# One core, attention and a dense branch: an instruction order recorded by engine clocks, and single score blocks for VectorE

## The chip, the cores and the metric

The kernel runs on one core of one Trainium2 chip. Its time is the device time of one execution in microseconds (us), the median of several executions. Five engines work beside each other, each through its own list of instructions in order: TensorE (PE: matmuls; PEld: its weight loads), ScalarE (ACT), VectorE (DVE), GpSimd (POOL) and SyncE (SP, which here only issues transfers). They wait for each other through semaphores. Matmuls write to PSUM, which has eight banks of 128 partitions by 512 float32 values; everything else lies in SBUF.

## The reference

`x` is 2048 x 512. It is normalised row by row to `xn`. Two branches start from `xn` and meet at the end:

```python
q = (xn @ wq)            # 32 heads of 16 columns
k, v = xn @ wk, xn @ wv  # one k and one v of 16 columns, shared by all heads
p = softmax(q @ k.T / 4) # for each head: 2048 queries x 2048 keys
s = (p @ v for all heads) @ wo
g = silu(silu(xn @ w1) @ w2)   # w1 512 x 1792, w2 1792 x 512
out = x + s * g
```

There are 32 x 2048 x 2048 exponentials. They are most of the work, since each head has only 16 columns.

## The kernel before, in words

**Tiles.** The queries are cut into 4 chunks `c` of 512, the heads into 8 sets `g` of four, the keys into 16 tiles `kt` of 128. The 32 pairs (c, g) are called groups here. One score tile (c, g, kt) consists of four blocks, one for each head of the set. A block holds 128 keys on the partitions and 512 queries along the row, so it fills one PSUM bank. In all there are 32 x 16 = 512 tiles, or 2048 blocks. The four heads of a set use the four quarters of TensorE's rows (`burst`, L509), so that blocks of different heads run at the same time.

**Two ways to an exponential.** A tile of the A kind goes through `psA0` and `psA1`, two banks each: two blocks at a time are read by one ScalarE instruction (`emit_E`, L568) that writes 128 x 1024 values into one of 11 slots of `pa_sb`. A tile takes two such instructions. A tile of the D kind goes through `psD`, also two banks: VectorE adds a constant and converts to int16 (`emit_P1`, L581), which gives the bit pattern of a bfloat16 close to the exponential. It also takes two instructions a tile. GpSimd then makes two more patterns from the four blocks (`emit_shift`, two `int64_add` at L592), and the three patterns, weighted, give a better exponential. So a D tile has to be multiplied with the values three times, an A tile once.

**The value product.** `emit_PV` (L628) multiplies four blocks of four heads at a time with the values, on the four quarters of TensorE's columns, into bank `psO`. I call such a set of four matmuls a quad. An A tile costs one quad, a D tile three. When a group is complete, VectorE transposes the bank (`gn1`, L663) and normalises it in three or four further instructions (`gn2` to `gn4`).

**The dense work.** The query projections (`q`), first layer (`h`), second layer (`z`) and output projection (`w`, `wp`) are 104 jobs of 3 to 14 matmuls that all use the one bank `psF`. After an `h` or `z` job ScalarE takes a tanh of the bank (`emit_tanh`, L817) and VectorE multiplies tanh and bank (L858); after the others VectorE reads the bank once (L403, L866, L875). The bank is free for the next job only then.

**The order.** `Sched.op` records each instruction for its engine and works out the semaphore waits. The order on each engine is the order in which Python calls `op`. Before the change, this follows a fixed pattern. The 346 A tiles are the units of the loop `for u in range(NU)` (L887). A unit records two ScalarE exponentials (a tanh may come before either), VectorE's small tasks as far as a budget `room` of 0.85 or 1.3 us goes (L893), and one D instruction (L897); the two halves of a D tile fall to two units in turn. For each half unit TensorE gets the score blocks of the next unit (`emit_S`; the D blocks directly behind the second A pair of the unit) and then either a part of a dense job or up to `cap` quads (L913 to L928). Jobs have due units (`spread`, L695). The counts are fixed ahead (L490 to L497): from unit 12 (`NFRONT`) on, each unit carries half a D tile, which gives 166 D tiles. The first 12 units have none, since `psD` and VectorE still serve the layer norm, the keys and the values there. After the loop the last quads are recorded, then the last output projection, whose sums lie in `psA` (L939 to L970).

Of the kernel before, what the change touches and what calls it, by code (L numbers as in the profile page):

```python
# [6 lines left out]
ALU = mybir.AluOpType  # L7
# [28 lines left out]
class Sched:  # L36

    def __init__(self):
        self.queues = {}
        self.done = {}
        self.clock = {}
        self.snap = {}
        self.last_w = {}
        self.readers = {}
        self.flagged = {}
        self.lanes = {}

    def op(self, eng, fn, reads=(), writes=(), lane=None):
        who = lane or eng
        if lane:
            self.lanes[lane] = eng
        n = self.done.get(who, 0)
        self.done[who] = n + 1
# [15 lines left out]
        for w in writes:  # L72
            if w in self.last_w:
                dep(*self.last_w[w])
            for f, m in self.readers.get(w, {}).items():
                dep(f, m)
        clk = self.clock.setdefault(eng, {})
# [61 lines left out]
def bass_recurrent_scan__grouped_kv_mqa__dense_activation_silu__prompt_kernel(  # L139
# [32 lines left out]
    LEAD = 1  # L172
    NFRONT = 12

    with ExitStack() as es:
# [38 lines left out]
        scr_i = sb("scr_i", [P, 8], I16)  # L214
        psA = [es.enter_context(nc.psum_tensor("psA0", [P, 1024], FP32)),
# [16 lines left out]
        def load_x(a, b, queue="sp"):  # L232
            op(queue, lambda e: e.dma_start(x_sb[:, a:b, :], xv[:, a:b, :]), writes=[("x", t) for t in range(a, b)],  # L233
               lane=f"lx{a}")
# [7 lines left out]
        op("sp", lambda e: e.dma_start(wq_sb[:], A_wq.rearrange("(dc p) n -> p dc n", p=P)), writes=["wq"], lane="lwq")  # L242
# [22 lines left out]
        def warm(n, bank, key):  # L265
# [4 lines left out]
            op("pe", f, reads=["zero"], writes=[key])  # L270
# [119 lines left out]
        def mm_Q(c, t, dcs=range(NDC)):  # L390
# [5 lines left out]
            op("pe", f, reads=xnT_keys(c) + ["wq"], writes=["F"])  # L396

        def evac_Q(c, t, eng):
# [3 lines left out]
            else:  # L402
                op("v", lambda e: e.tensor_scalar(dst, psF[:, :], QSCALE, None, op0=ALU.mult), reads=["F"], writes=[("qT", c % 2, t)])  # L403
# [86 lines left out]
        units, dtiles = [], []  # L490
        for c in range(NC):
            for g in range(NG):
                n = 0
                while n < NKT and NFRONT + 2 * (len(dtiles) + n + 1) <= len(units) + (NKT - n - 1) - LEAD:
                    n += 1
                units += [(c, g, kt) for kt in range(NKT - n)]
                dtiles += [(c, g, kt) for kt in range(NKT - n, NKT)]  # L497
        NU = len(units)
        first_unit = [min(u for u, k in enumerate(units) if k[0] == c) for c in range(NC)]
        for u, k in enumerate(units):  # L500
            phase = (u - NFRONT) % 2
            m = (u - NFRONT) // 2
            d = dtiles[m] if u >= NFRONT and m < len(dtiles) else None
            units[u] = dict(phase=phase, pair=m, A=[[(k, 0), (k, 1)], [(k, 2), (k, 3)]][::1 if phase == 0 else -1],
                            D=[] if d is None else [(d, 0), (d, 1)] if phase == 0 else [(d, 2), (d, 3)])

        def score(e, blk, ap):
            (c, g, kt), i = blk
            return e.matmul(ap, lhsT=kT_sb[g % 2][32 * i:32 * i + 32, kt * P:(kt + 1) * P],  # L509
                            rhs=qT_sb[32 * i:32 * i + 32, c % 2, g // 2, :],  # L510
                            start=True, stop=True, tile_position=(32 * i, 0))

        def burst(items, writes):
            rd = set()
            for ((c, g, kt), i), _ in items:
                if ("q", c, g // 2) not in jst["q"]:
                    raise ValueError(f"no q for {c}, {g}")
                rd.add(("qT", c % 2, g // 2))
                rd.add(("kT", 1, kt // 2, i) if g % 2 else ("kT", 0, kt // 2 if kt else "first"))

            def f(e):
                for blk, ap in items:
                    r = score(e, blk, ap)
                return r
            op("pe", f, reads=sorted(rd, key=str), writes=writes)

        def emit_S(u, which):

            un = units[u]
            burst([(blk, psA[which][:, 512 * k:512 * k + 512]) for k, blk in enumerate(un["A"][which])], ["A%d" % which])  # L530
            if which == 1 and un["D"]:
                burst([(blk, psD[:, 512 * k:512 * k + 512]) for k, blk in enumerate(un["D"])], ["D", "D1"])

        NGRP = NC * NG
        pend = [[] for _ in range(NGRP)]
        left = [0] * NGRP
        for un in units:
            for blk in un["D"]:
                left[blk[0][0] * NG + blk[0][1]] += NPH
            for h in range(2):  # L540
                for blk in un["A"][h]:
                    left[blk[0][0] * NG + blk[0][1]] += 1
        npv = [[0] * 4 for _ in range(NGRP)]
        tot = [[0] * 4 for _ in range(NGRP)]
        for un in units:
            for blk in un["D"]:
                tot[blk[0][0] * NG + blk[0][1]][blk[1]] += NPH
            for h in range(2):
                for blk in un["A"][h]:
                    tot[blk[0][0] * NG + blk[0][1]][blk[1]] += 1  # L550

        step_now = [0]
        state = dict(g=0, o_step=-1, half=0)

        def fresh(key):
            for q in pend:
                for p in q:
                    if p["key"] == key:
                        raise ValueError(f"{key} is still to be read, step {step_now[0]}")

        def emit_E(u, h):
            un = units[u]
            if not un["A"][h]:
                return
            sl = (2 * u + h) % NPA
            step_now[0] = 2 * u
            fresh(("pa", sl))
            op("a", lambda e: e.activation(pa_sb[:, sl, :], psA[h][:, :], ACT.Exp, scale=ESCALE),  # L568
               reads=["A%d" % h], writes=[("pa", sl)])
            for k, (kk, i) in enumerate(un["A"][h]):  # L570
                gi = kk[0] * NG + kk[1]
                pend[gi].append(dict(i=i, kt=kk[2], v=0, ap=pa_sb[:, sl, 512 * k:512 * k + 512], key=("pa", sl),
                                     ready=2 * u + h))

        def emit_P1(u):
            un = units[u]
            if not un["D"]:
                return
            sl, h = un["pair"] % NPD, un["phase"]
            fresh(("ph", 0, sl, h))  # L580
            op("v", lambda e: e.tensor_scalar(ph_sb[0][:, sl, 1024 * h:1024 * h + 1024], psD[:, :],  # L581
                                              float(PH_ONE + PH_BIAS), 0.0, op0=ALU.add, op1=ALU.max),
               reads=["D", "D1"], writes=[("ph", 0, sl, h)])
            for k, (kk, i) in enumerate(un["D"]):
# [423 lines left out]
```

## Time and profile before

| | |
|---|---|
| median of three runs | 696.19 us (695.96 to 696.57) |
| span of the profiled execution, first to last instruction | 695.3 us |
| granted TensorE clock, mean | 1.000 |
| ScalarE, busy | 677.0 us (97%) |
| TensorE, busy by the records | 677.3 us (97%) |
| VectorE, busy | 552.4 us (79%) |
| GpSimd, busy | 352.3 us (51%) |
| ScalarE exponentials (L568) | 692, mean 1233 ns |
| VectorE pattern instructions (L581) | 332, mean 1221 ns |
| GpSimd shifts (L592) | 332, mean 1038 ns |
| tanh (L817) | 72, mean 824 ns |

The whole execution is a little longer than the span of its instructions. The busy time of an engine is the time covered by at least one of its records. Records overlap: on ScalarE and TensorE an instruction starts while the one before it is still in the pipeline, so the number of instructions times the mean duration is more than the busy time. What one more instruction costs is read from the distance between the ends, or the starts, of neighbours.

### The profile page before, as it was taken

What the parts mean: (1) busy time and instruction counts of PE and PEld (TensorE: products, weight loads), DVE (VectorE), ACT (ScalarE), POOL (GpSimd) and SP (SyncE); (2) the same over time, 40 slices, a digit from 0 to 9 for tenths busy, and PEclk for the clock granted to TensorE, in tenths of its full rate; (3) what the DMA queues carried; (4) which work ended last, traced back from release to release, by engine and by line L of the source; (5) the groups of instructions that cost most, each with busy time, mean ns of one, the idle gap of its engine ahead of it and who ended that gap; (6) DMA issues with size and microseconds to landing.
All of it is one profiled execution on the core that took longest, in us unless ns stands there. A gap on an engine that the chain in (4) does not pass through costs nothing.

```text
span 695.3 us, 14435 instructions
## 1 busy us (share of the span) xinstructions
PE 677.3 (97%) x6279; PEld 183.0 (26%) x6279; DVE 552.4 (79%) x639; ACT 677.0 (97%) x773; POOL 352.3 (51%) x361
## 2 busy tenths in 40 slices
PE   8999999999999999999999999999999999999996
PEld 3432222222222222222222222222222222222221
DVE  6778778887778877888778787887878888787884
ACT  5899999999999999999999999999999999999995
POOL 4134545545455555555555555455545555555452
PEclk9999999999999999999999999999999999999999
DMA  9300000000000000000000000000000000000000
GB/s 296 112 5 1 1 2 1 1 1 2 1 1 8 9 1 9 8 2 1 1 1 10 8 8 1 10 1 1 1 2 1 8 17 2 9 1 2 1 1 31
DMA packets 7887, 10.13 MB, mean 15 GB/s; under 512 B 1744, under 2 KB 7120, under 8 KB 7824
## 3 DMA queue, kind: packets, MB, share of 16 engines
q1 hardware_dynamic: 6656, 5.15, 2.4%
q0 software_dynamic: 736, 3.67, 1.5%
q8 instruction: 49, 0.80, 0.5%
q10 hardware_dynamic: 432, 0.39, 0.2%
q14 instruction: 14, 0.11, 0.1%
HBM read 6.85 MB, written 2.10 MB: 13 GB/s over the span
## 4 chain that ended last, share of the span: by engine, by line
ACT 93%; PE 4%; DVE 1%; DMA 1%; POOL 0%; SPq 0%; issue 0%; DVEq 0%
ACT pa_sb L568 87%; ACT t_sb L817 5%; DMA wq_sb<-in_A_wq_dram 1%; PE psA L509 1%; PE psF L268 1%; PE psD L316 1%; DVE stats_sb L277 0%; PE psO L628 0%; POOL rstd_sb L286 0%; PE psD L351 0%; PE psF L351 0%; PE psA L939 0%; SPq L233 0%; PE psF L771 0%; DVE wq_sb L960 0%
## 5 line engine op out<-in xcount | busy, mean ns | idle before, releaser
L568 ACT ACTIVATE pa_sb<-psA 128x1024 bf16<-128x1024 f32 x692 | 660.5, 1233 | 4.3 <-PE psA L509 3.8
L592 POOL INT64_ADD ph_sb<-ph_sb x332 | 340.5, 1038 | 306.0 <-DVE ph_sb L581 306.0
L581 DVE TENSOR_SCALAR ph_sb<-psD 128x1024 int16<-128x1024 f32 x332 | 405.3, 1221 | 97.6 <-PE psD L509 96.5
L628 PE MATMUL psO<-ph_sb,vaug_sb 128*32 128x512 bf16 x1992 | 236.4, 384 | 0.0
L628 PE MATMUL psO<-pa_sb,vaug_sb 128*32 128x512 bf16 x1384 | 208.9, 384 | 0.4 <-ACT pa_sb L568 0.4
L509 PE MATMUL psA<-qT_sb,kTa_sb 32*128 32x512 bf16 x700 | 135.7, 384 | 4.5 <-ACT pa_sb L568 3.4
L509 PE MATMUL psA<-qT_sb,kTb_sb 32*128 32x512 bf16 x684 | 132.7, 385 | 3.5 <-ACT pa_sb L568 2.5
L509 PEld LDWEIGHTS psA<-qT_sb,kTa_sb 32*128 32x128 bf16 x700 | 32.9, 90 | 152.4 <-ACT pa_sb L568 146.5
L509 PEld LDWEIGHTS psA<-qT_sb,kTb_sb 32*128 32x128 bf16 x684 | 32.1, 91 | 152.0 <-ACT pa_sb L568 150.1
L628 PEld LDWEIGHTS psO<-ph_sb,vaug_sb 128*32 128x32 bf16 x1992 | 53.0, 94 | 58.1 <-issue 45.1
L759 PE MATMUL psF<-xnT_sb,w_sb 128*128 128x512 bf16 x224 | 67.8, 384 | 0.0
L509 PE MATMUL psD<-qT_sb,kTb_sb 32*128 32x512 bf16 x340 | 66.0, 384 | 0.0
L771 PE MATMUL psF<-w_sb,u_sb 128*128 128x512 bf16 x224 | 65.0, 384 | 0.0
L509 PE MATMUL psD<-qT_sb,kTa_sb 32*128 32x512 bf16 x324 | 62.8, 385 | 0.0
L628 PEld LDWEIGHTS psO<-pa_sb,vaug_sb 128*32 128x32 bf16 x1384 | 49.2, 94 | 43.9 <-issue 33.3
L817 ACT ACTIVATE t_sb<-psF 128x512 bf16<-128x512 f32 x72 | 59.3, 824 | 0.0
L858 DVE SCALAR_TENSOR_TENSOR u_sb<-t_sb,psF 128x512 bf16<-128x512 bf16 x56 | 38.3, 684 | 20.6 <-ACT t_sb L817 20.6
L268 PE MATMUL psF<-zero_sb 128*128 128x512 bf16 x100 | 34.3, 413 | 1.2 <-DVE zero_sb L252 1.2
L663 DVE STREAM_TRANSPOSE otr_sb<-psO 128x512 f32<-128x512 f32 x32 | 22.9, 715 | 5.4 <-PE psO L628 5.0
L771 PEld LDWEIGHTS psF<-w_sb,u_sb 128*128 128x128 bf16 x224 | 14.1, 97 | 25.6 <-issue 21.5
L393 PE MATMUL psF<-xnT_sb,wq_sb 128*128 128x512 bf16 x64 | 19.2, 384 | 1.1 <-DMA wq_sb<-in_A_wq_dram 1.1
L759 PEld LDWEIGHTS psF<-xnT_sb,w_sb 128*128 128x128 bf16 x224 | 12.7, 97 | 25.4 <-issue 24.7
(83 smaller groups left out, 222.6 us busy)
## 6 DMA issues: line engine op xcount, KB each, us to landing
w_sb<-in_B_w_dram POOLq DMA_DIRECT2D x2, 1792.0 KB, 12.9
out_dram<-ob_sb SPq DMA_DIRECT2D x15, 128.0 KB, 1.7
x_sb<-in_A_x_dram SPq DMA_DIRECT2D x3, 512.0 KB, 8.2
wq_sb<-in_A_wq_dram SPq DMA_DIRECT2D x1, 512.0 KB, 7.9
wop_sb<-in_A_wo_dram SPq DMA_DIRECT2D x1, 512.0 KB, 10.3
x_sb<-in_A_x_dram SPq DMA_DIRECT2D x2, 128.0 KB, 2.9
x_sb<-in_A_x_dram ACTq DMA_DIRECT2D x2, 128.0 KB, 3.1
kTb_sb<-kTa_sb SPq DMA_DIRECT2D x16, 16.0 KB, 3.0
```

What stands on the lines that cost most here:

```text
L268: r = e.matmul(bank, lhsT=zero_sb[:, 0:P], rhs=zero_sb[:, :], start=True, stop=True)
L393: r = e.matmul(psF[:, :], lhsT=wq_sb[:, dc, t * P:(t + 1) * P], rhs=xnT_sb[:, dc, c * NQ:(c + 1) * NQ], start=(dc == 0), stop=(dc == NDC - 1))
L509: return e.matmul(ap, lhsT=kT_sb[g % 2][32 * i:32 * i + 32, kt * P:(kt + 1) * P], rhs=qT_sb[32 * i:32 * i + 32, c % 2, g // 2, :], start=T ...
L568: op("a", lambda e: e.activation(pa_sb[:, sl, :], psA[h][:, :], ACT.Exp, scale=ESCALE), reads=["A%d" % h], writes=[("pa", sl)])
L581: op("v", lambda e: e.tensor_scalar(ph_sb[0][:, sl, 1024 * h:1024 * h + 1024], psD[:, :], float(PH_ONE + PH_BIAS), 0.0, op0=ALU.add, op1=A ...
L592: op("gp", lambda e, j=j: e.int64_add(ph_sb[j][:, ss, :].bitcast(I64), ph_sb[0][:, sl, :].bitcast(I64), PH_SHIFT[j] * 0x0001000100010001), ...
L628: r = e.matmul(psO[32 * i:32 * i + 32, :], lhsT=vaug_sb[:, p["v"], p["kt"], :], rhs=p["ap"], start=s0, stop=s1, tile_position=(0, 32 * i), ...
L663: op("v", lambda e: e.transpose(otr_sb[:, sl, :], psO[:, :]), reads=["O"], writes=[("otr", sl)])
L759: r = e.matmul(psF[:, :], lhsT=w1_sb[:, dc, ft * P:(ft + 1) * P], rhs=xnT_sb[:, dc, c * NQ:(c + 1) * NQ], start=(dc == 0), stop=(dc == NDC ...
L771: r = e.matmul(psF[:, :], lhsT=u_sb[:, (tt // 4) % 2, ft, (tt % 4) * P:(tt % 4 + 1) * P], rhs=w2_sb[:, ft, :], start=(ft == 0), stop=(ft = ...
L817: op("a", lambda e: e.activation(t_sb[:, sl, :], psF[:, :], ACT.Tanh, scale=0.5 if jb[0] == "h" else 0.25), reads=["F"], writes=[("t", sl)])
L858: op("v", lambda e: e.scalar_tensor_tensor(out=dst, in0=t_sb[:, sl, :], scalar=1.0, in1=psF[:, :], op0=ALU.add, op1=ALU.mult), reads=["F", ...
```

## The change

The fixed units and the list of D tiles are gone. `Sched` gets a clock for each engine: `model` says for each recorded instruction when it starts and ends, from constants in microseconds, and `at` keeps that for every instruction. The recorder uses these clocks only to choose what to record next; on the chip the order is fixed, and semaphores guard every dependence as before.

The new loop goes from one pair of score blocks for ScalarE to the next. It works out how much time TensorE has until ScalarE needs the next pair (`need`), fills this with up to four matmuls of a job or up to four quads, and calls `score_run`. That records the A pair and behind it, if `psD` is free within `SLIP` = 0.25 us, a D pair; the D tile is taken at that moment from the end of the current group, or of the next group. If no D pair is recorded, `fill_F` may put one single score block into `psF`, if no job holds that bank. VectorE converts this block alone (`exp_F`), and when the four blocks of the tile are done, GpSimd makes the two further patterns. Up to `NF` = 14 tiles go this way. Their patterns lie in `x_sb`, rows 0 to 11, whose content is no longer needed then; so the rows of `x` that the final additions need are loaded again, one row tile at a time, by 16 transfers on SP's queue (`load_xr`). `advance_v` chooses VectorE's next instruction: a small task or the D conversion, whichever can start first; a task may go ahead of a D conversion unless that makes the conversion miss an earlier ScalarE release, and after `AGE` = 2 us a task goes ahead anyway. The first 12 tiles keep their order; only their quads are chosen by the clocks. The last output projection is unchanged.

The diff, cut to its core:

```diff
+    SWITCH, FLY, SEM = 0.104, 0.172, 0.048
...
+    def ready(self, eng, reads=(), writes=()):
+        return max([self.at[d] for d in self.deps(eng, reads, writes).items()], default=0.0)
+
+    def pe_next(self, mode):
+        return self.pe_last + self.pe_len + (self.SWITCH if mode != self.pe_mode else 0.003)
...
+        if eng == "a":
+            n = cost or 512
+            t = max(r, self.free["a"], self.act_end - 0.428)
+            self.free["a"] = t
+            self.act_end = max(t + 0.3 + n / 1200.0, self.act_end + 0.0635 + n / 1200.0)
+            return self.act_end + self.SEM
+        t = max(r, self.free[eng] - (0.084 if eng == "v" else 0.0))
+        self.free[eng] = t + (cost or 0.4)
+        return self.free[eng] + self.SEM
...
-    LEAD = 1
     NFRONT = 12
+    XR = 12
+    LEAD, LEAD_END, SLIP, AGE, AGE1, MARGIN = 3, 3, 0.25, 2.0, 1.2, 0.0
+    NF, F_FROM, F_LEFT, F_LATE, DENSE_END, HOLD, F_BEHIND = 14, 0.05, 9, 10, 0.95, 10, 12
...
+        pe_ph = [x_sb[:, 4 * j:4 * j + 4, :].rearrange("p a b -> p (a b)").bitcast(I16) for j in range(NPH)]
...
-                while n < NKT and NFRONT + 2 * (len(dtiles) + n + 1) <= len(units) + (NKT - n - 1) - LEAD:
...
-            units[u] = dict(phase=phase, pair=m, A=[[(k, 0), (k, 1)], [(k, 2), (k, 3)]][::1 if phase == 0 else -1],
-                            D=[] if d is None else [(d, 0), (d, 1)] if phase == 0 else [(d, 2), (d, 3)])
...
+        def fill_A(tile, rows, k):
+            burst([((tile, i), psA[k][:, 512 * n:512 * n + 512]) for n, i in enumerate(rows)], ["A%d" % k])
...
+        def exp_F(tile, i, nth):
+            d = op("v", lambda e: e.tensor_scalar(pe_ph[0][:, 512 * i:512 * i + 512], psF[:, :],
+                                                  float(PH_ONE + PH_BIAS), 0.0, op0=ALU.add, op1=ALU.max),
+                   reads=["F"], writes=[("x", i)], cost=0.69)
+            owe(tile[0], i, tile[1], 1, pe_ph[0][:, 512 * i:512 * i + 512].bitcast(BF16), ("x", i), K.at[d])
+            if nth == 3:
+                for j in range(1, NPH):
+                    d = op("gp", lambda e, j=j: e.int64_add(pe_ph[j][:, :].bitcast(I64), pe_ph[0][:, :].bitcast(I64),
+                                                            PH_SHIFT[j] * 0x0001000100010001),
+                           reads=[("x", i) for i in range(4)], writes=[("x", 4 * j + i) for i in range(4)], cost=1.03)
+                    for r in range(4):
+                        owe(tile[0], r, tile[1], 1 + j, pe_ph[j][:, 512 * r:512 * r + 512].bitcast(BF16), ("x", 4 * j + r), K.at[d])
...
+                cand = sorted((p for p in pend[gi] if p["at"] <= t), key=lambda p: p["at"])
...
+        def behind(by=0):
+            return jst["slots"] + by < need_slots[-1] * (progress() - F0) / (F1 - F0)
...
+        def load_xr(tt):
+            if tt < NT:
+                op("sp", lambda e: e.dma_start(x_sb[:, XR + tt % 4, :], xv[:, tt, :]), writes=[("x", XR + tt % 4)],
+                   lane=f"xr{tt % 4}")
...
+                now = [(x, tk) for x, tk in cand if x <= first + 0.01]
+                now.sort(key=lambda p: (p[1]["kind"] != "gn1", p[1]["kind"] in ("gn2", "gn3", "gn4", "add"), p[1].get("born", 0.0)))
+                pick = now[0][1] if now else None
+                if pick is not None and d < first + pick["cost"] and first - pick.setdefault("born", first) < (AGE1 if pick["kind"] == "gn1" else AGE):
+                    if meets(d + 1.27) < meets(first + pick["cost"] + 1.22):
+                        pick = None
+                if pick is not None:
+                    tasks.remove(pick)
+                    pick["run"](pick)
+                elif d < t:
+                    exp_D(dst["tile"], dst["rows"], dst["half"])
+                    dst["filled"] = False
+                    dst["half"] ^= 1
+                    if not dst["half"]:
+                        dst["tile"] = None
...
+        def score_run(t):
+            t = max(t, releases()[0])
+            want, rd = None, None
+            if not dst["filled"]:
+                want = next_D(t)
+            if want is not None and dst["half"]:
+                rd = other(drows[0])
+            merge = want is not None and K.ready("pe", [], ["D", "D1"]) <= t + SLIP
+            if ast["tile"] is None:
+                gi = group_A()
+                tile = ast["tile"] = (gi, left[gi].pop(0))
+                rows = ast["rows"] = [0, 1] if rd is None else other(rd) if merge else rd
+                second = False
+            else:
+                tile, rows = ast["tile"], other(ast["rows"])
+                second = True
+            fill_A(tile, rows, state["n"] % 2)
+            if merge:
+                if rd is None:
+                    left[want[0]].remove(want[1])
+                    plan_D(want[0])
+                    dst["tile"] = want
+                    rd = other(rows)
+                drows[dst["half"]] = dst["rows"] = rd
+                dst["filled"] = True
+                burst([((want, i), psD[:, 512 * k:512 * k + 512]) for k, i in enumerate(rd)], ["D", "D1"])
+            else:
+                fill_F(t, rows)
+            while jst["tanh"] and K.ready("a", ["F"], [("t", state["nt"] % 2)]) <= K.act_end - 0.33:
+                emit_tanh()
+            exp_A(tile, rows)
+            if second:
+                ast["tile"] = None
+
+        def other(rows):
+            return [i for i in range(4) if i not in rows]
+
...
+        def fill_F(t, rows):
+            if jst["busy"] or jst["part"] or K.ready("pe", [], ["F"]) > t + SLIP:
+                return
+            if est["tile"] is None:
+                if est["n"] >= NF or any(held(("x", k)) for k in range(12)) or progress() < F_FROM:
+                    return
+                ga = group_A()
+                gi = ga if len(left[ga]) >= F_LEFT else ga + 1
+                if gi >= NGRP or len(left[gi]) < 2 or ("q", gi // NG, (gi % NG) // 2) not in qdone:
+                    return
+                if behind(F_BEHIND):
+                    return
+                tile = (gi, left[gi].pop())
+                plan_D(gi)
+                est.update(tile=tile, todo=[0, 1, 2, 3], nth=0)
+                est["n"] += 1
+            late = F_late()
+            i = next((i for i in est["todo"] if i not in rows), est["todo"][0] if late else None)
+            if i is None:
+                return
+            est["todo"].remove(i)
+            burst([((est["tile"], i), psF[:, :])], ["F"])
+            jst["busy"] = True
+            tasks.append(dict(kind="e", jb=None, tile=est["tile"], i=i, nth=est["nth"], reads=["F"], writes=[("x", i)], cost=0.69, run=evac))
+            est["nth"] += 1
...
+        while state["g"] < NGRP or jst["n"] < len(jobs) or tasks:
+            t = max(now, min(K.pe_next("col"), K.pe_next("full")))
...
+            if more:
+                need = K.act_end + (0.49 if jst["tanh"] else 0.0) + 0.9175 - 1.153 - 0.45 - MARGIN
+                slots = min(4, int((need - t - K.SWITCH) / 0.2163))
+            else:
+                slots = 4
...
+                full = blocked or sum(held(("pa", k)) for k in range(NPA)) >= HOLD
+                can = job_ready(t)
+                if can and not full and (jst["part"] or behind() or not more):
+                    did = emit_job(slots)
+                if not did:
+                    did = emit_PV(t + 0.08, slots)
+                if not did and can:
+                    did = emit_job(slots)
+            if more and not held(("pa", state["n"] % NPA)):
+                if slots >= 2 and not did:
+                    filler(1)
+                score_run(t)
+                now = 0.0
+            elif not did:
```

## The prediction

> **What bounds the kernel now.** I read the page from the top: busy shares, then the chain that ended last, then the costliest groups.
>
> ```profile
> PE 677.3 (97%) x6279; PEld 183.0 (26%) x6279; DVE 552.4 (79%) x639; ACT 677.0 (97%) x773; POOL 352.3 (51%) x361
> ...
> ACT 93%; PE 4%; DVE 1%; DMA 1%; POOL 0%; SPq 0%; issue 0%; DVEq 0%
> ACT pa_sb L568 87%; ACT t_sb L817 5%; DMA wq_sb<-in_A_wq_dram 1%; PE psA L509 1%; PE psF L268 1%; PE psD L316 1%; DVE stats_sb L277 0%; PE psO L628 0%; POOL rstd_sb L286 0%; PE psD L351 0%; PE psF L351 0%; PE psA L939 0%; SPq L233 0%; PE psF L771 0%; DVE wq_sb L960 0%
> ...
> L568 ACT ACTIVATE pa_sb<-psA 128x1024 bf16<-128x1024 f32 x692 | 660.5, 1233 | 4.3 <-PE psA L509 3.8
> ...
> L581 DVE TENSOR_SCALAR ph_sb<-psD 128x1024 int16<-128x1024 f32 x332 | 405.3, 1221 | 97.6 <-PE psD L509 96.5
> ```
>
> Two engines show 97%, but the chain runs through ScalarE for 93% of the span. The stretch 40 to 686 us settles it: ScalarE is busy 645.91 of 646 us.
>
> ```profile
> 40.00:686.00 646.00, 637.96 (x5960) 166.34 (x5958) 518.77 (x555) 645.91 (x738) 340.48 (x332) 1.00 0.01 4
> ```
>
> The columns are PE, PEld, DVE, ACT, POOL, each with its count. The chain lists runs of exponentials such as 33 in 30.26 us: 0.917 us each; a tanh between two adds about 0.49 us (one run ends at 55.60, the next begins at 56.09). So before = 39.9 us of start, 665 x 0.917 = 609.8, 72 x 0.49 = 35.3, and 9.3 us from the last exponential (686.1) to the end, in sum 694.3 of 695.3 us. Time falls by 0.917 us for each ScalarE exponential removed, as long as TensorE still feeds ScalarE.
>
> TensorE's 97% says less. Matmul records last 384 ns, but neighbours start about 0.217 us apart:
>
> ```profile
> 303.64 0.38 PE L628 MATMUL psO<-pa_sb,vaug_sb 128*32 128x512 bf16 x2
> ...
> 303.87 0.38 PE L628 MATMUL psO<-pa_sb,vaug_sb 128*32 128x512 bf16 x2
> ...
> 304.07 0.39 PE L628 MATMUL psO<-ph_sb,vaug_sb 128*32 128x512 bf16 x4
> ...
> 304.50 0.39 PE L509 MATMUL psA<-qT_sb,kTb_sb 32*128 32x512 bf16 x2
> ...
> 304.83 0.39 PE L628 MATMUL psO<-ph_sb,vaug_sb 128*32 128x512 bf16 x2
> ```
>
> 304.50 to 304.83 is the change from score rows to value columns: 0.33 us, that is 0.11 us over 0.217. [...]
>
> **What the change moves.** *ScalarE.* Let D be the tiles through `psD`, 14 those through `psF`, A the rest; A + D + 14 = 512. Before, 692 exponentials stand beside 332 D conversions: two for each, and 28 unpaired ones at both ends. One D conversion lasts 1.22 us; with filling the bank and signalling, conversions start at least 1.70 us apart in the trace. That is more than one exponential with a tanh (1.41 us) plus the 0.25 us the change lets TensorE wait, so one D pair for two exponentials stays the best rate. If it is held, 2A = 4D + 28, hence D = 161.3, A = 336.7 and 673.3 exponentials: the 14 tiles save 18.7, not 28, because a shorter loop has room for fewer D pairs. That is 17.1 us. Each D pair that misses its turn costs a third of an exponential (0.31 us).
>
> *VectorE: how many misses?* In the 646 us it works 518.8 us, of which 404 are D conversions and 115 other tasks. A single block costs what the nearest row shows, another conversion of 128x512 from the same bank, 0.685 us (L403): 56 x 0.685 = 38.4 us. After: 322 x 1.221 + 115 + 38 = 546 of about 629 us, 87% instead of 80%. Where does it wait now?
>
> ```profile
> DVE ph_sb L581 <- PE psD L509: 96.5, 177, 0.8
> ...
> DVE u_sb L858 <- ACT t_sb L817: 20.6, 38, 0.6
> ...
> PEld psD L509 <- DVE ph_sb L581: 2.7, 11, 0.3
> ```
>
> 177 times it is idle for 0.55 us before a conversion; TensorE waited for it only 11 times, 2.7 us. Between conversions there are 1.834 - 1.221 = 0.61 us, and a task of 0.69 us overruns by 0.08 us. 56 of the 177 free gaps take the single blocks and some 120 stay, which reset the drift. So conversions miss only where tasks come in clusters (the end of a group, a tanh). Bounds: 0 misses and 50, one for every sixth D pair. I take 14, nearer to zero, because of the 120 gaps: that gives A = 339, D = 159, 678 exponentials, 14 saved, 12.8 us.
>
> *Bank F.* In order of time, from a job's first matmul to the end of the instruction that frees the bank, a first-layer job holds it 3.6 us (56 jobs), a second-layer job 11.9 (16), an output projection 2.6 (16), a query job 2.5 (15 in the loop): 474 us of 646, with 102 gaps, 161 us. A single block needs 0.39 for the matmul, 0.69 for the conversion and some 0.4 of waiting for VectorE, 1.5 us: 84 us for 56. They fit, and second-layer jobs in larger parts give more room. I count on all 14 tiles.
>
> *TensorE.* A tile moved from A to D or F loses two score bursts and gains two quads. Loop before: 665 bursts, about 825 quads, 568 dense matmuls, 2058 x 0.217 = 447 us, plus two mode changes a burst, 665 x 0.21 = 140: 587 of 646. After: as many matmuls, 651 bursts, 447 + 137 = 584 of about 633: spare 49 us. A single block runs on row quarters that the A pair leaves free, beside it: nothing, or 0.217 x 56 = 12 us of that spare where it can't. ScalarE tolerates a late burst by some 0.2 us (records average 1.233, while the first of a run, which starts late, lasts 1.02). Three quads in a row are late by about 0.15 us. I allow 1 us of ScalarE idle in place of 0.1; bounds 0 and the slower rival.
>
> *GpSimd, SP, start, tail.* Seven more DVE tiles (173 against 166) are 14 shifts x 1.04 = 15 us on an engine idle 306 us before its shifts; if that cover went, the three pattern slots would fill and D would miss. The 16 reloads of `x` land in about 2.9 us like the 128 KB loads at the start, SP has only 15 stores in the loop, and each row is loaded four additions ahead: nothing; uncovered, 2.9 us for one addition, of which only the last could delay the end. The four head loads stand behind no other transfer. Start (same order) and tail (same last projection) at 0, bounds -2 and +6 us, three dense jobs left over at about 2 us.
>
> Sum: 695.3 - 12.8 + 1 = 683.5 us of span. The median, 696.19, lies 0.85 above the span: **684.4 us**, 1.7% faster.
>
> **Rivals.** *1. TensorE becomes the bound (slower).* The place is the D burst behind the A pair: up to 0.25 us of waiting for VectorE's conversion blocks everything behind it on TensorE, the quads above all. 318 bursts at 0.25 us are 80 us, 31 over the spare 49. Decision point: 0.154 us of mean wait. If the mean is 0.21 us, 67 - 49 = 18 us of quads come late, the 11 `pa_sb` slots fill, and ScalarE waits: 684.4 + 18 = 702. For it: VectorE at 87%, tasks that overrun. Against it: only 2.7 us of such waits now, and the wait is skipped when it would be over 0.25 us. [...]
>
> *2. The change does little.* Jobs hold bank F, only 4 tiles go through it: 692 - 5.3 + 4.7 for 14 misses, 691 exponentials, 695.3 - 0.6 + 1 = 696 us, 696.5 with the 0.85. For it: 474 us of 646 are taken. Against: 161 us of gaps.
>
> *3. No misses.* 673.3 exponentials and no idle: 695.3 - 17.1 = 678.2, 679 as median; with a tail shortened by 2 us, 677.
>
> *4. Many misses,* 50 of them: 690 exponentials, 2 saved, 1.8 - 1 = 0.8 us gained: 695.4 us.
>
> **Numbers.** The forecast (0 to 35 misses, 1 to 4 us of ScalarE idle) spans 679 to 692 and has 0.57; no misses or better 0.15; little or many misses, 692 to 698, 0.11; TensorE the bound, above 698, 0.17. A measurement of this kernel can tell about 0.2%, 1.4 us, from no change: the middle case splits into 0.04 faster, 0.04 same and 0.03 slower. So faster 0.57 + 0.15 + 0.04 = 0.76, same 0.04, slower 0.20. The range 676 to 700 leaves out about 0.03 below and 0.13 above.
>
> **What would show it.** Right: 674 to 684 exponentials, about 318 D conversions, 56 single conversions of 0.69 us in the F bank, ScalarE still busy without gaps between 40 us and its last exponential, ends 0.917 us apart, VectorE's waits for D bursts down from 96.5 to 50 to 80 us. Wrong: ScalarE idle by tens of us with TensorE as releaser (rival 1), far fewer than 56 single conversions (rival 2), under 300 D conversions (rival 4), or more than 12 us behind the last exponential.

## The result, and the profile after

The changed kernel takes 701.74 us (700.40 to 703.53, four runs) against 696.08 us; the ratio is 1.0082, with a 95% interval of 1.0065 to 1.0100. It is slower by 0.8%. The forecast was 684.4 us with a range of 676 to 700. The profiled execution, one of 700.4 us, has a span of 698.4 us. Ratios leave out runs that are over 1.5% longer than the fastest of their kernel, which is one run of e1 (710.8 us).

First the page: busy shares, ScalarE and granted clock in 40 slices, the chain that ended last, and groups.

```profile
PE 650.9 (93%) x6151; PEld 185.8 (27%) x6236; DVE 560.6 (80%) x669; ACT 674.8 (97%) x767; POOL 361.8 (52%) x367
...
ACT  5999899999999999999999989999999999999995
...
PEclk9999799999999999999999989999999999999999
...
ACT 72%; PE 15%; DVE 10%; issue 1%; DMA 0%; POOL 0%; DVEq 0%
...
L589 ACT ACTIVATE pa_sb<-psA 128x1024 bf16<-128x1024 f32 x686 | 652.9, 1159 | 9.4 <-PE psA L559 7.2
...
L600 DVE TENSOR_SCALAR ph_sb<-psD 128x1024 int16<-128x1024 f32 x314 | 382.6, 1218 | 100.4 <-PE psD L559 93.4
...
L624 DVE TENSOR_SCALAR x_sb<-psF 128x512 int16<-128x512 f32 x48 | 32.6, 679 | 1.4 <-PE psF L559 1.4
...
L709 DVE TENSOR_TENSOR onb_sb<-otr_sb,rcp_sb 128x256 bf16<-128x256 f32 x32 | 21.9, 686 | 0.6
```

The change does what it says: 48 single conversions (12 tiles of the 14 allowed), 686 exponentials on ScalarE instead of 692. But the chain lies on ScalarE for 72% of the span instead of 93%, and the clock, which was full in every slice before, dips in two slices, the same two in which ScalarE shows an 8.

Where the time went, by the trace. On ScalarE, exponentials end 0.917 us apart and a tanh adds 0.49 us when nothing is late. After 40 us, the changed kernel exceeds this by 9.9 us at 35 places (before: 0.3 us at 2); this is the idle time of ScalarE meant below. Six exponentials fewer are -5.5 us, the idle is +9.6, one more exponential done by 40 us is -0.9, the tail +0.1: in sum +3.3, and the spans differ by 3.1 us. Of the 9.9 us, 6.4 lie in two stretches, from 70 and from 408 us. The first of them, by busy time (columns PE, PEld, DVE, ACT, POOL, then granted clock):

```profile
60.00:70.60 10.60, 8.89 (x79) 2.26 (x76) 8.38 (x11) 10.60 (x14) 4.25 (x6) 1.00 0.00 1
70.70:80.90 10.20, 9.87 (x58) 1.78 (x55) 6.15 (x8) 7.05 (x9) 6.07 (x6) 0.50 0.01 2
81.00:91.00 10.00, 9.79 (x105) 2.79 (x108) 8.31 (x9) 9.95 (x12) 5.01 (x5) 1.00 0.00 0
```

From 70.7 to 80.9 us the clock is at half, TensorE does 58 matmuls instead of about 100, and ScalarE is busy 7.05 of 10.20 us. The clock record gives 10.24 us for this stretch, from 70.65 us on, and 6.83 us for the second, from 408.57 us on; the two lengths differ by 3.41 us. The four runs show how this varies: mean clocks of 0.986, 0.985, 0.983 and 0.981 belong to 700.4, 700.8, 702.6 and 703.5 us.

The timeline just ahead of the first stretch shows what TensorE lacked:

```profile
65.71 0.61 PE L783 MATMUL psF<-xnT_sb,w_sb 128*128 128x512 bf16 x2
...
66.57 0.62 PE L663 MATMUL psO<-pa_sb,vaug_sb 128*32 128x512 bf16 x8
66.72 1.22 DVE L600 TENSOR_SCALAR ph_sb<-psD 128x1024 int16<-128x1024 f32 x1 [0.54 <-PE psD L559]
66.74 0.76 ACT L840 ACTIVATE t_sb<-psF 128x512 bf16<-128x512 f32 x1
67.12 0.39 PE L559 MATMUL psA<-qT_sb,kTa_sb 32*128 32x512 bf16 x2
...
67.86 0.70 DVE L692 STREAM_TRANSPOSE otr_sb<-psO 128x512 f32<-128x512 f32 x1
68.47 0.39 PE L559 MATMUL psA<-qT_sb,kTa_sb 32*128 32x512 bf16 x2 [0.96 <-ACT pa_sb L589]
68.49 0.65 DVE L866 SCALAR_TENSOR_TENSOR u_sb<-t_sb,psF 128x512 bf16<-128x512 bf16 x1
```

It is the end of a group. The last quads run at 66.57, so `psO` is closed until its transposition ends at 68.56. A job's last matmuls start at 65.71, and VectorE reads its sum from 68.49 on, so `psF` is held until 69.14. `psD` is being converted until 67.94, the A banks belong to ScalarE. For 1.1 us there is hardly a bank into which TensorE may write, and a zero matmul has no place either. Between 40 and 684 us there are 18 holes of over 0.6 us, ten over 0.9; before there were 2 and none. All but the last of the 18 lie at the end of a group. In seven of them `psO` came free 0.4 to 0.8 us before the hole ended: there the recorded order, not a bank, set the last part.

I count how empty TensorE gets like this: its busy share in any 3.4 us (the difference of the two lengths), where a matmul counts as its record less 0.17 us (384 ns last, 217 apart), and a missing record as its weight load tells. Before, the emptiest such stretch is 58% busy. After, five separate ones lie under 45%. The two stretches at half clock did not follow these five, though, but 3.4 us that were 54 and 52% busy; e12 comes back to this.

### The profile page after: what moved, and what is told of

Read it like the earlier page. It is cut to its first block, busy times and chain, and to the rows that moved or that the text cites. A ratio compares the mean times of both kernels' runs of the same rounds, so it can differ in the third digit from the quotient of the medians.

```text
span 698.4 us, 14374 instructions
## 1 busy us (share of the span) xinstructions
PE 650.9 (93%) x6151; PEld 185.8 (27%) x6236; DVE 560.6 (80%) x669; ACT 674.8 (97%) x767; POOL 361.8 (52%) x367
## 4 chain that ended last, share of the span: by engine, by line
ACT 72%; PE 15%; DVE 10%; issue 1%; DMA 0%; POOL 0%; DVEq 0%
ACT pa_sb L589 68%; PE psO L663 5%; PE psA L559 5%; DVE ph_sb L600 5%; ACT t_sb L840 4%; DVE stats_sb L328 1%; DVE x_sb L624 1%; PE psF L783 1%; PE psF L795 1%; PE psD L559 1%; DVE onb_sb L709 1%; DVE ob_sb L851 1%; PE psF L319 0%; DMA x_sb<-in_A_x_dram 0%; DVE otr_sb L692 0%
## 5 line engine op out<-in xcount | busy, mean ns | idle before, releaser
L589 ACT ACTIVATE pa_sb<-psA 128x1024 bf16<-128x1024 f32 x686 | 652.9, 1159 | 9.4 <-PE psA L559 7.2
L610 POOL INT64_ADD ph_sb<-ph_sb x314 | 325.5, 1048 | 295.6 <-DVE ph_sb L600 295.6
L600 DVE TENSOR_SCALAR ph_sb<-psD 128x1024 int16<-128x1024 f32 x314 | 382.6, 1218 | 100.4 <-PE psD L559 93.4
L663 PE MATMUL psO<-ph_sb,vaug_sb 128*32 128x512 bf16 x1884 | 206.7, 387 | 0.0
L663 PE MATMUL psO<-pa_sb,vaug_sb 128*32 128x512 bf16 x1372 | 181.2, 386 | 0.3 <-DVE vaug_sb L435 0.3
L559 PE MATMUL psA<-qT_sb,kTa_sb 32*128 32x512 bf16 x704 | 138.8, 391 | 12.0 <-ACT pa_sb L589 10.1
L783 PE MATMUL psF<-xnT_sb,w_sb 128*128 128x512 bf16 x188 | 61.0, 391 | 5.8 <-issue 5.0
L624 DVE TENSOR_SCALAR x_sb<-psF 128x512 int16<-128x512 f32 x48 | 32.6, 679 | 1.4 <-PE psF L559 1.4
L630 POOL INT64_ADD x_sb<-x_sb x24 | 25.0, 1054 | 5.1 <-DVE x_sb L624 5.1
L692 DVE STREAM_TRANSPOSE otr_sb<-psO 128x512 f32<-128x512 f32 x32 | 22.7, 709 | 6.0 <-PE psO L663 5.9
L663 PE MATMUL psO<-x_sb,vaug_sb 128*32 128x512 bf16 x144 | 25.2, 387 | 0.0
L709 DVE TENSOR_TENSOR onb_sb<-otr_sb,rcp_sb 128x256 bf16<-128x256 f32 x32 | 21.9, 686 | 0.6
```

Source lines behind the costliest of these rows:

```text
L589: d = op("a", lambda e: e.activation(pa_sb[:, sl, :], psA[k][:, :], ACT.Exp, scale=ESCALE), reads=["A%d" % k], writes=[("pa", sl)], cost=2 ...
L600: d = op("v", lambda e: e.tensor_scalar(ph_sb[0][:, sl, 1024 * half:1024 * half + 1024], psD[:, :], float(PH_ONE + PH_BIAS), 0.0, op0=ALU. ...
L610: d = op("gp", lambda e, j=j: e.int64_add(ph_sb[j][:, ss, :].bitcast(I64), ph_sb[0][:, sl, :].bitcast(I64), PH_SHIFT[j] * 0x0001000100010001),
L624: d = op("v", lambda e: e.tensor_scalar(pe_ph[0][:, 512 * i:512 * i + 512], psF[:, :], float(PH_ONE + PH_BIAS), 0.0, op0=ALU.add, op1=ALU. ...
L630: d = op("gp", lambda e, j=j: e.int64_add(pe_ph[j][:, :].bitcast(I64), pe_ph[0][:, :].bitcast(I64), PH_SHIFT[j] * 0x0001000100010001), rea ...
L663: r = e.matmul(psO[32 * i:32 * i + 32, :], lhsT=vaug_sb[:, p["v"], p["kt"], :], rhs=p["ap"], start=s0, stop=s1, tile_position=(0, 32 * i), ...
```

## The experiments

Two theories were tried first. Theory G: the holes let the clock drop to half, and that costs most of what was lost. Rival M: the clock is a side show, missed D turns and late bursts cost. Later runs ask what the single blocks are worth, and what the other idle time of ScalarE is. "Slow stretch" below means a stretch at half clock.

### e1: the old kernel without its zero matmuls

```diff
         def filler(n, active):
 
+            return
             if not jst["busy"] and not jst["part"]:
```

> The kernel before, with the zero matmuls of its loop left out (75 of 115; the start and the last 6 units keep theirs). Its array work in the emptiest 3.4 us falls from about 0.44 to 0.2 to 0.3. Theory G (holes in TensorE's work let the clock drop, and that costs time): the mean granted clock falls below 0.995, with slow stretches near 85, 149, 190 or 460 us, and the time rises to 697.5 to 704 us. Rival M (the clock is not what costs; missed D pairs and late bursts are): the zero matmuls are dead weight, 695.5 to 696.5 us, whatever the clock does.

Measured: 704.38 us (697.51 to 710.81, ten runs), ratio 1.0100 (1.0069 to 1.0132). The median lies just above the range given for G. Time follows the clock from run to run: 697.5 us at 0.994, 700.3 at 0.988, 703.8 at 0.982, 706.7 at 0.974; that is 9.2 us for 0.020. The profiled execution has the 692 exponentials and 332 conversions of before, and four stretches at half clock; the clock by slices, and one of the stretches:

```profile
PEclk9969989998999999999999999999999999999999
```

```profile
80.00:100.00 20.00, 17.35 (x148) 4.01 (x146) 14.51 (x16) 18.46 (x22) 10.25 (x10) 0.86 0.00 1
```

Nothing but the fillers is gone (the trace has 38 zero matmuls instead of 115), and of 9.0 us of idle 8.6 lie in and just behind the stretches at half clock. G is right about the clock, in an order that has nothing to do with the recorder; M's 696 us is out. Stretches at half clock began here after 3.4 us in which TensorE was 34 to 45% busy. The changed kernel has 48 zero matmuls.

### e2: no single blocks

```diff
-    NF, F_FROM, F_LEFT, F_LATE, DENSE_END, HOLD, F_BEHIND = 14, 0.05, 9, 10, 0.95, 10, 12
+    NF, F_FROM, F_LEFT, F_LATE, DENSE_END, HOLD, F_BEHIND = 0, 0.05, 9, 10, 0.95, 10, 12
```

> The changed kernel with NF = 0: no tile goes through psF, the recorded order has 696 ScalarE exponentials instead of 686. Theory G with the recorder's order as the cause of the holes: slow stretches remain, time 701.7 + 10 x 0.917 = 711 us, 706 to 714. Rival F (the single blocks hold the bank at group ends and so make the holes): no slow stretches, 6 to 9 us of ScalarE idle gone, 701 to 705 us.

Measured: 705.19 us (701.22 to 707.56), ratio 1.0126 (1.0091 to 1.0161), just above rival F's range and below G's; the profiled execution has two slow stretches and 5.7 us of idle. So the recorder makes holes without the single blocks too, and F, which wants them as the cause, is out. But the time is 6 us under the 711 of G, since the slow stretches here are shorter (10.2 us in all against 17.1) and ScalarE idles 4.2 us less. The run doesn't separate more than this.

### e3: keep a bank free at the end of a group

```diff
@@ fill_F
+            if state["g"] < group_A() and t >= gdone[state["g"]] and owed[state["g"]] <= NKEEP:
+                return
@@ loop
-                can = job_ready(t)
+                can = job_ready(t) and not (more and not jst["part"] and state["g"] < group_A() and t >= gdone[state["g"]] and owed[state["g"]] <= NKEEP)
...
-                if slots >= 2 and not did:
-                    filler(1)
+                if slots - did >= 1 and K.active(t) < 0.6:
+                    filler(slots - did)
```

`NKEEP` is 16; `K.active` sums the array work recorded for the last 3.41 us, where a matmul on a quarter of the array counts a quarter.

> The changed kernel, with no job or single block started in the F bank when at most 16 blocks of the group are still to be multiplied (so that a job fills the gap while the group's bank is read), and zero matmuls in free slots when the array work of the last 3.4 us is under 0.6. 684 exponentials. Theory G: no slow stretch before the last exponential, mean clock at least 0.992, ScalarE idle 2 to 5 us instead of 9.9, time 690 to 695 us. Rival M: TensorE's extra work makes bursts late, 698 to 704 us.

Measured: 694.99 us (694.74 to 695.88, ten runs), ratio to before 0.9983 (0.9974 to 0.9993): 6.7 us less than the changed kernel, with 684 exponentials; the two fewer make 1.8 of the 6.7. No stretch at half clock lies before the last exponential, the mean clock is 0.998 or more in all ten runs, and the emptiest 3.4 us is 47% busy. G again. But ScalarE still idles 6.3 us, at 36 places, more than the 2 to 5 expected: late bursts at full clock, the part that M names. At 12 of them (3.0 us) VectorE had a task of L709's kind (here at L715) that took 0.9 to 1.25 instead of 0.42 us within the 6.5 us before; that it caused the late burst in each is not shown. The clock by slices and the exponentials:

```profile
PEclk9999999999999999999999999999999999999999
...
L595 ACT ACTIVATE pa_sb<-psA 128x1024 bf16<-128x1024 f32 x684 | 648.9, 1149 | 6.1 <-PE psA L565 4.1
```

### e4: tasks with two inputs not beside GpSimd's shifts

```diff
-                cand = [(max(tv, K.ready("v", tk["reads"], tk["writes"])), tk) for tk in tasks]
+                cand = [(max(tv, K.ready("v", tk["reads"], tk["writes"]), K.free["gp"] + 0.05 if tk["kind"] in ("gn3", "add") and K.free["gp"] - tv < 2.2 else 0.0), tk) for tk in tasks]
```

> The changed kernel, with VectorE's two-input tasks (L709 and the additions) not chosen while GpSimd shifts. 688 exponentials. If the stretched tasks (686 ns against 526 before) cause the missed D pairs: L709 falls to 430 to 500 ns on average, missed turns on the chip fall, 697 to 700 us. If they only move waits about: 701 to 705 us, two exponentials more (1.8 us) and the same slow stretches.

Measured: 698.96 us (698.20 to 703.46), ratio 1.0057 (1.0031 to 1.0083). The edit did not do what it was for: 17 of 32 instances of the task still meet a shift and it averages 649 ns. So this run says nothing of what a meeting costs, though its time lies in the first range. Slow stretches are there: 698.2 us belongs to a clock of 0.993, 703.5 to 0.983.

### e5 and e8: each half of e3 alone

e5 has the second hunk of e3's loop (more zero matmuls) alone, e8 the first alone (no new job near the end of a group). The hunk in `fill_F`, which holds back single blocks, is in neither.

> The changed kernel with the second half of e3 alone: zero matmuls in free slots when the array work of the last 3.4 us is under 0.6, jobs and single blocks as in the changed kernel. 686 exponentials. Theory G with the holes lying where both free banks are taken (the group's bank is being read, a job's sum waits in F): the fillers have nowhere to go, slow stretches remain, 698 to 703 us. Rival: missing fillers alone made the slow stretches, then none is left and the time is 692 to 696 us.

> The changed kernel with the first half of e3 alone, for jobs only: no job is begun in the F bank when at most 16 blocks of the group are left. 686 exponentials, 9 tiles through psF. The recorded order still has ten stretches of 3.4 us with array work under 0.37 (nothing fills the slots in which no job may begin). Theory G: slow stretches remain, 698 to 704 us. Rival (the free bank alone does it): 691 to 696 us.

Measured: e5 697.61 us (695.58 to 699.31), ratio 1.0019 (1.0007 to 1.0031); e8 702.47 us (699.79 to 704.35), ratio 1.0073 (1.0052 to 1.0095). Both profiles show three slow stretches; those of e5 are the shortest of any run, 3.4 us each, and its time lies 0.4 us under the range given for G and above the rival's. Against the changed kernel, with the same 686 exponentials, more fillers alone bring 4.1 us and the free bank alone none. e3 brings 4.9 beside its two exponentials, and only there are the slow stretches gone. So the fillers do most, and to keep the clock up it takes both: the mean clock is 0.998 or more in all runs of e3, 0.991 to 0.998 in e5 and 0.980 to 0.988 in e8.

### e6, e7, e9: fewer exponentials, fewer late bursts

e6 is e3 with `NF` = 10. e7 is e3 with `NKEEP` = 8, `AGE` = 4.0 and a price for tasks that meet a shift; e9 is e7 without that price.

```diff
                 cand = [(max(tv, K.ready("v", tk["reads"], tk["writes"])), tk) for tk in tasks]
+                for x, tk in cand:
+                    if tk["kind"] in ("gn3", "add"):
+                        e = K.free["gp"]
+                        tk["cost"] = 0.43 + max(0.0, (e - x if e - x <= 1.03 else e - 1.03 - x) if x < e and e - x < 2.06 else 0.0)
```

> e3 with at most 10 single-block tiles instead of 14 (it took 11). The order has 682 exponentials instead of 684, since more D pairs find their turn, and no stretch of array work under 0.38. If exponentials at 0.917 us set the time once the clock stays up: 695.0 - 1.8 = 693.2 us, 692.3 to 694.2. If TensorE is the bound there: 695 to 697 us.

> e3 with 8 blocks as its limit, an age of 4 us, and a price in the recorder's clock for VectorE's two-input tasks that meet GpSimd's shifts. 682 exponentials, two stretches of array work at 0.33. If wrong prices of these tasks make the 6.3 us of ScalarE idle of e3 (late D bursts that hold TensorE): idle falls to 3 to 4 us and the time is 690 to 693 us, plus 2 to 4 us if one of the two stretches drops the clock. If the idle has another source: 693 to 698 us.

> e7 without the price for tasks that meet GpSimd's shifts. Also 682 exponentials; three stretches of array work at 0.25 to 0.33 instead of two. If the price is what took ScalarE's idle from 6.3 us (e3) to 1.6 (e7): idle is 4 to 7 us again, VectorE's L709 averages 0.65 to 0.75 us instead of 0.52, time 692 to 697 us. If the other two limits did it: 689 to 691 us.

Measured: e6 692.77 us, ratio 0.9950 (0.9935 to 0.9965), 682 exponentials and 6.1 us of idle: two exponentials less gave 2.2 us, close to the 1.8 by 0.917. e7 689.41 us, 0.9907 (0.9884 to 0.9929), also 682 exponentials, idle 1.6 us; one of its four runs, at a clock of 0.995, took 692.3. e9 693.13 us, 0.9942 (0.9924 to 0.9961): idle 5.1 us, but 2.9 of that in one slow stretch from 628 us, and the tail, from the last exponential to the end, is 11.4 us instead of 10.1. Outside the stretch e9 idles 2.2 us, hardly more than e7. Its time lies in the range given for the price, but through that stretch and the tail. So my reason for e7 falls: the price shortens L709's task (523 ns against 602) and changes the order, but the fall from 6 to 2 us came with the other two limits. Which of the two did it is open.

### e10: the best version, and e11: what the single blocks are worth

e10 is e7 with `NKEEP` = 6, `AGE` = 6.0 and fillers below 0.5; e11 is e7 with `NF` = 0.

> e7 with tasks allowed to wait 6 us instead of 4 before they go ahead of a D conversion, a limit of 6 blocks and fillers below 0.5. The order has 678 exponentials and all 14 tiles, one stretch of array work at 0.33. Exponentials set the time once the clock stays up and late bursts are few: 689.4 - 4 x 0.917 = 685.7 us, 685 to 688. If waiting tasks hold the F bank or the group's bank too long: above 689 us.

> e7 with NF = 0. 694 exponentials instead of 682. The single blocks alone are worth 12 x 0.917 = 11 us where the clock stays up: 700 us, 698 to 702. If they cost as much in late bursts as they save: 690 to 696 us.

Measured: e10 684.29 us (683.81 to 685.33), ratio to before 0.9827 (0.9812 to 0.9841), 1.7% faster than before, 2.5% faster than the changed kernel, and 0.7 us under the range given. Its exponentials (from the page's groups), the task that was stretched (from the groups by line), and busy time by stretches:

```profile
L595 ACT ACTIVATE pa_sb<-psA 128x1024 bf16<-128x1024 f32 x678 | 644.2, 1193 | 3.6 <-PE psA L565 2.8
```

```profile
L715 DVE TENSOR_TENSOR onb_sb<-otr_sb,rcp_sb 128x256 bf16<-128x256 f32 x32 | 15.4, 480 | 0.3
```

```profile
40.00:100.00 60.00, 55.76 (x540) 16.30 (x542) 50.35 (x57) 60.00 (x71) 31.95 (x31) 1.00 0.04 11
100.00:400.00 300.00, 287.08 (x2805) 78.39 (x2801) 249.74 (x281) 299.85 (x346) 167.73 (x164) 1.00 0.02 5
400.00:673.00 273.00, 264.75 (x2613) 72.52 (x2605) 228.51 (x261) 272.99 (x310) 156.38 (x152) 1.00 0.03 9
```

All 14 tiles, 678 exponentials, the clock full, and ScalarE almost without gaps: ends are late by 0.5 us in all. e11 takes 698.67 us, ratio 1.0034 (1.0022 to 1.0046), with 694 exponentials, 0.3 us of idle and no slow stretch. Against e7 the single blocks are worth 9.3 us, of 11 forecast.

### e12: narrow fillers

```diff
-                warm(n, psF[:, :], "F")
...
+                        r = e.matmul(psF[0:32, :], lhsT=zero_sb[:, 0:32], rhs=zero_sb[:, :], start=True, stop=True,
+                                     tile_position=(0, 0))
```

(and in the same way for the fillers into `psO`)

> The kernel before, with each of the 75 zero matmuls of its loop narrowed from 128 to 32 columns of the array: as long in time, a quarter of the array. If the gate goes by the share of the array that works (how I weighed the emptiest 3.4 us): nearly as without them (e1), slow stretches, a mean clock under 0.995 and 697.5 to 709 us. If it goes by the time in which TensorE is busy at all: no slow stretch, 696 us as before.

Measured: 696.34 us (695.72 to 703.37, eleven runs), ratio 1.0008 (0.9988 to 1.0027). Ten runs show a clock of 0.998 or more and the time of before; one fell to 0.987 and 703.4 us. So narrow fillers keep the clock up nearly as well as full ones, against ten runs at 0.994 or less without any (e1). By this run alone the time in which TensorE is busy at all would be what counts, and not the share of the array, by which e3 to e11 were designed. By busy time the kernels sort like this (profiled executions, 42 to 668 us; one of e1's four stretches at half clock begins at 33 us):

| kernel | separate 3.4 us stretches under 45% busy | stretches at half clock |
|---|---|---|
| before, e3, e6, e10, e12 | 0 | 0 |
| e11 | 1 | 0 |
| e7 | 2 or 3, by how missing records are filled in | 0 |
| changed kernel | 5 | 2 |
| e1, e9 | 3, 4 | 4, 1 |
| e2, e4 | 5, 5 | 2, 2 |
| e5, e8 | 7, 8 | 3, 3 |

Busy time alone does not sort them all: e9 has four such stretches and one at half clock, e7 two or three and none. The places in the changed kernel's trace say the same. The 3.4 us directly ahead of its two stretches at half clock are 54 and 52% busy, while the five separate ones under 45%, 37 to 42% busy at their emptiest, are followed by full clock. The array share, which counts each matmul by the part of the array that it uses, with quarters that run at the same time added up, does not part them either when it is taken over any 3.4 us: it is 38 and 36% directly ahead of the two stretches, which hold quarter matmuls only, and falls to 25 to 32% in the five. And by busy time no 3.41 us of e12's profiled execution is under 58%, as in the kernel before, yet one of its eleven runs fell to 0.987. "Nearly as without them" was a wrong forecast from the array share, with ten of eleven runs at 0.998 or more. So the runs show that the fillers keep the clock up (0.998 or more in the kernel before, 0.994 or less in e1), and not how empty TensorE must be for it to drop.

## Why the prediction was wrong

**What bounds the kernel, and the price of an exponential: right.** ScalarE set the time before, and 0.917 us an exponential held wherever the clock did (e3 to e6; e7 to e10: 4 x 0.917 = 3.7 us, with 1.1 us less idle and a tail shorter by 0.4, 5.2 in the profiled spans). The step to the median, 0.85 us, was too small: an execution lies 2.0 us above its own span (700.4 against 698.4). One reading of the trace was off: conversions start at least 1.65 us apart in the trace before, not 1.70, which is no more than the 1.66 it was set against.

**"I allow 1 us of ScalarE idle" is the step that failed first, with 9.9 measured. The idle grew by 9.6 instead of 1, which is 8.6 of the 14.9 us by which the span was missed.** I summed TensorE's spare time over the whole loop, 49 us, and took it as cover everywhere. The spare is not where it is needed: at a group's end hardly a bank is free, whatever the sum says. And I looked at the granted clock only as a figure of 1.000, without asking what kept it there. The old loop holds jobs back near a group's end (L741), lets a group end at one place of a unit only, and records a job or a zero matmul for the two half units after it (L922 to L924). The recorder dropped this rule: its order has 48 zero matmuls where the old one has 115. e3 holds back jobs and fills again and wins 6.7 us, 1.8 of them by two exponentials; e1 shows that in the old kernel, too, the zero matmuls are worth 8 us. I had costed them at nothing without naming them. How empty TensorE must be for the clock to drop is not shown: the changed kernel's two stretches at half clock follow 3.4 us that were 54 and 52% busy.

**"I take 14 misses": 30.** Between neighbouring D fills lie two A bursts 293 times, three 15 times, four to six 5 times, which makes 30 too many. Since more misses are a third of an exponential each, 16 of them are 5.3 exponentials, 4.9 us. Free gaps were there, 163 of them, but the tasks came in clusters at a group's end, where L692, L700, L709 and L718 follow each other: 24 of the 30 misses lie in the 7.2 us behind a group's transposition, while groups come some 20 us apart. Besides, 8 conversions waited for a pattern slot, since a D tile of the next group cannot be multiplied before the current group is done. What each of the two cost was not separated. The waits from 40 to 690 us:

```profile
DVE ph_sb L600 <- PE psD L559: 93.4, 163, 1.7
...
PEld psD L559 <- DVE ph_sb L600: 4.4, 11, 0.8
DVE otr_sb L692 <- PE psO L663: 5.9, 4, 2.8
DVE ph_sb L600 <- PE psO L663: 5.7, 8, 2.1
```

VectorE's idle ahead of D bursts hardly fell (93.4 us; 50 to 80 was forecast): the tasks did not go into those gaps. L709's task, which reads two operands from SBUF, grew from 526 to 686 ns. 27 of its 32 records meet a shift of GpSimd (21 before) and last 0.41 to 1.26 us (0.42 to 0.80 before); those that meet none last 0.41 to 0.43. The prediction had left this out, and why the records that meet a shift last longer is not shown. What it costs in time was not separated (e4, e9).

**"I count on all 14 tiles": 12.** Worth 2.7 exponentials, 2.4 us. With the 8.6 and the 4.9 this is 15.9 us; one more exponential done by 40 us takes 0.9 off. The number moves with the order: 11 tiles in e3, 13 in e5 and e7, 14 in e10. What holds it down is not shown.

**One D pair for two exponentials as the best rate: right.** No D pair came after a single burst. **Price of a single block:** 679 ns against 685 forecast, right. **Reloads of `x`, GpSimd, tail:** hidden, as forecast (tail 9.4 against 9.3 us).

**Rival 1** gave 702 us, near the result, but by another mechanism: it wanted D bursts that wait 0.21 us each, 67 us, and the waits of TensorE for conversions are 5.7 us (4.4 and 1.3) against 2.7 before. Its number was luck. Late bursts are real at full clock, about 3.5 us here and 6.3 in e3.

What stays open: what exactly lets the clock drop (neither the busy time nor the array share of any 3.4 us parts the places, and one of e7's four runs dropped to 0.995); which of the limits took the late bursts out of e7; and what the meeting of L709 with the shifts costs by itself.

## What to carry to other kernels

Spare time of an engine is worth something only where it lies: look for the emptiest few microseconds, not at the sum, above all where a buffer is handed over and every other buffer is taken. What kept the clock up here were zero matmuls at the right places, on the whole array (0.998 or more in all runs of e3) or on a quarter of it (ten of eleven runs of e12); the old kernel without those of its loop had 0.994 or less (e1). When an order is made anew, list what the old order did that looks like nothing (zero matmuls, rules that hold work back at a boundary) and take one of them out of the old kernel to see its price. A granted clock of 1.000 is a result that something pays for.

## What the runs showed of the hardware

Stretches at half clock lasted 10.24 and 6.83 us in the changed kernel and 3.4 us each in e5. They came after 3.4 us in which TensorE was busy for 54 and 52% of the time (changed kernel) and 34 to 45% (e1), while five emptier 3.4 us of the changed kernel, 37 to 42% busy, were followed by full clock. The same kernel differs by up to 10 us from run to run (e1: 697.5 to 707.5), with mean clocks of 0.994 to 0.974. Zero matmuls on a quarter of the array held the clock nearly as well as those on the whole (e12: ten of eleven runs at 0.998 or more). And the changed kernel's first stretch at half clock, which began 2.2 us after a hole of 1.1 us, took about 4 us from ScalarE.
